# Layer 2 of two feed-forward layers: combined weights made earlier, seven products in every tile, and a new plan

## The chip, the cores and the metric

The kernel runs on one core of one Trainium2 chip. The metric is the device time of one execution in microseconds (us). The engines are TensorE (PE, matrix products; PEld is its weight load), VectorE (DVE), ScalarE (ACT), GpSimd (POOL) and SyncE (SP), which issues almost all DMAs in one in-order queue.

## The reference, cut to what matters

```python
# attention: 2 x 8 heads, 768 positions, 64 wide; a local window of 16 on either side,
# and 24 block summaries (max of k, mean of v over 32 positions)
a = np.exp(scores_all); a = a / (np.sum(a, axis=-1, keepdims=True) + 1e-09)
x = np.matmul(a, v_all)            # as 1536 tokens x 512
# layer 1 (called layer 0 in the code)
h = x @ w_in                       # 512 x 2048
x = (h * (1.0 / (1.0 + np.exp(-1.702 * h)))) @ w_out
# layer 2 (layer 1 in the code)
h = x @ w_in2
out = (h * np.cos(h)) @ w_out2
```

## The kernel before

**Tiles and steps.** The 1536 tokens are three tiles of 512 (`U`). Each layer goes through its tiles one after the other, and each tile in 16 steps f of 128 hidden columns. A step computes h on TensorE (`ff_h`, L881), passes it through a gate chain of ScalarE and VectorE (`ff_gate`, L996; 2 links in layer 1, 7 in layer 2), splits the result into g hi and g lo, and multiplies it by w_out into four accumulators (`ff_out`, L1093), two steps behind. Every fp32 product is three fp32r passes over hi and lo parts (hi x hi, lo x hi, hi x lo). The attention of the second and third tile (units 4 to 11 of 128 positions) is laid between the steps of layer 1's first two tiles; at the start, 13 dummy products and more behind the first units keep TensorE busy (`fill`, L383).

**Weights.** Each weight row m is 1 MB of raw 64-bit words for two blocks. `w_load` (L725) brings it into one of the buffers rawA, rawB, rawC; `convert` (L737) makes the two blocks' hi and lo parts: scale (L740, ACT), low (L746, DVE), join (L750, DVE), and for each block hi (L767, ACT) and lo (L771, DVE). Layer 1's 16 rows are converted during its first tile, layer 2's 16 rows during its third.

**Combined products.** For the second and third tile of layer 2 (`WINO`), two steps are taken together as a pair: `ff_wino` (L913) computes their h by a seven-product scheme for 2 x 2 blocks in place of eight, each product six matmuls of 256 columns (L939). It takes blocks of w and x (1 to 4) and combined ones: sums of weight blocks, and sums t1 to t4 of x blocks (`prep_wino`, L836). Sums of the products ("h copy" on ACT, L962; seven "h sum" on DVE, L964) give the four blocks of h. The first tile of layer 2 has plain steps.

**Where the weight sums come from.** In `convert` of the eight rows with w_in blocks, `sums_of` (L787) follows the join: four sums (L794, DVE), hi (L798, ACT), lo (L799, DVE), all in the row's own raw buffer, and a 1 MB DMA to a DRAM scratch (`sd`, L802). So the raw buffer is free for the next row's load only when that DMA has landed. In layer 2 each pair loads its 1 MB back (L925).

**Buffers.** xf0 and xf1 hold a tile's x or output ([128, 4, 512]); `xb` holds seven slots of split x. rawC holds the attention's k, q, v (`win`) until the last unit. `stage` and `spare` take the two buffers of the ring "wc" from layer 2's second tile on.

**Order.** All work is recorded as `Op`s; `order_of` (L271) sorts them with estimated durations and a table of priorities (`BONUS`), and each engine runs its instructions in that order, waiting on semaphores.

## Time and profile before

| what | us |
|---|---|
| three runs | 601.88, 603.9, 604.45; median 603.9 |
| the profiled execution, its time | 602.34 |
| its span, first to last instruction | 600.6 |
| time around the span | 1.74 |
| TensorE busy in the span | 580.6 (97%) |
| TensorE's mean granted clock | 0.995 of full speed |

A profile tells of one execution. Busy shares are averages over stages with different limits: what a change is worth is read from the waits in its stage. The stages are: start and first attention units to about 32 us, layer 1's first tile to 147, its second to 230, its third to about 337, then layer 2's three tiles of some 80 us each.

### The profile page before, as it was taken

Reading aid. Unit: us, or ns where it says so; the run is one execution under the profiler, and the core shown is the slowest. Engines: PE = TensorE matmul, PEld = TensorE weight load, DVE = VectorE, ACT = ScalarE, POOL = GpSimd, SP = SyncE. Lnnn points to the kernel's source line nnn. Section 1 sums busy time; section 2 is a strip of 40 time slices with the busy share of each in tenths; the row PEclk is TensorE's granted clock in tenths of the full one; section 3 lists DMA queues with packets and bytes.
Section 4 is the critical chain, followed back from the end, with each engine's and each line's share of the span. In section 5 each row is a group of like instructions: output and inputs, shape, how many; then the busy total and the mean of one; then the engine's idle time right before and its main releaser. Section 6 shows DMA issues by size and latency. Waiting matters only on the chain.

```text
span 600.6 us, 9453 instructions
## 1 busy us (share of the span) xinstructions
PE 580.6 (97%) x3628; PEld 479.4 (80%) x3633; DVE 431.0 (72%) x879; ACT 362.5 (60%) x733; POOL 29.9 (5%) x30
## 2 busy tenths in 40 slices
...
GB/s 326 395 344 244 196 198 266 217 108 175 8 73 80 36 0 141 211 210 204 207 220 210 280 1 1 0 1 0 113 204 105 71 76 135 141 136 76 1 2 70
DMA packets 27789, 82.30 MB, mean 137 GB/s; under 512 B 10336, under 2 KB 15456, under 8 KB 20576
## 3 DMA queue, kind: packets, MB, share of 16 engines
...
q14 instruction: 17, 0.14, 0.1%
q10 hardware_dynamic: 144, 0.13, 0.1%
...
## 4 chain that ended last, share of the span: by engine, by line
PE 62%; DVE 16%; DMA 15%; ACT 4%; issue 2%; SPq 1%; POOL 0%; DVEq 0%
PE acc L1108 30%; PE h_ps L894 19%; PE h_ps L939 8%; DMA raw<-in_w_dram 7%; DMA sd<-raw 5%; DMA vy<-in_vext_dram 2%; PE x_ps L541 2%; DVE g L1041 2%; DVE w L771 2%; DVE spare L964 1%; DVE gt L1033 1%; DVE raw L746 1%; DVE h_ps L964 1%; DVE raw L799 1%; PE s_ps L512 1%
## 5 line engine op out<-in xcount | busy, mean ns | idle before, releaser
L1108 PE MATMUL acc<-g,w 128*128 128x512 f32 x1155 | 279.6, 391 | 2.5 <-DVE g L1041 2.5
L1108 PEld LDWEIGHTS acc<-g,w 128*128 128x128 f32 x1155 | 213.6, 188 | 47.1 <-DVE g L1041 4.2
L894 PE MATMUL h_ps<-xb,w 128*128 128x512 f32 x768 | 187.8, 395 | 4.9 <-DVE gt L1009 2.8
L894 PEld LDWEIGHTS h_ps<-xb,w 128*128 128x128 f32 x768 | 143.5, 189 | 39.0 <-DVE gt L1009 5.1
L1037 ACT CAST g<-gt 128x512 fp32r<-128x512 f32 x96 | 59.3, 617 | 47.6 <-PE acc L1108 41.8
L1041 DVE TENSOR_TENSOR g<-gt,g 128x512 fp32r<-128x512 f32 x96 | 66.9, 698 | 27.6 <-ACT g L1037 27.3
L939 PE MATMUL h_ps<-xb,sums 128*128 128x256 f32 x384 | 52.6, 284 | 1.8 <-DVE h_ps L964 1.8
L939 PEld LDWEIGHTS h_ps<-xb,sums 128*128 128x128 f32 x384 | 49.2, 191 | 4.3 <-DVE h_ps L964 2.7
L1025 ACT ACTIVATE gt<-gt 128x512 f32<-128x512 f32 x48 | 30.2, 630 | 36.5 <-DVE gt L1021 36.4
L1003 ACT ACTIVATE gt<-h_ps 128x512 f32<-128x512 f32 x48 | 28.7, 597 | 34.5 <-PE h_ps L894 21.0
L1005 ACT ACTIVATE gt<-h_ps 128x512 f32<-128x512 f32 x48 | 28.6, 597 | 33.5 <-DVE g L1041 22.7
L771 DVE TENSOR_TENSOR w<-wc,w 128x512 fp32r<-128x512 f32 x64 | 46.9, 742 | 1.5 <-ACT w L767 1.5
L740 ACT ACTIVATE wc<-raw 128x1024 f32<-128x1024 f32 x32 | 36.8, 1155 | 14.5 <-DMA raw<-in_w_dram 8.8
L1033 DVE SCALAR_TENSOR_TENSOR gt<-gt,h_ps 128x512 f32<-128x512 f32 x48 | 32.8, 682 | 16.4 <-ACT gt L1029 16.4
L767 ACT CAST w<-wc 128x512 fp32r<-128x512 f32 x64 | 37.9, 619 | 8.9 <-DVE wc L750 4.7
L939 PE MATMUL h_ps<-xb,w 128*128 128x256 f32 x288 | 41.2, 284 | 1.5 <-DVE spare L964 1.2
L750 DVE SCALAR_TENSOR_TENSOR wc<-wc,raw 128x1024 uint32<-128x1024 uint32 x32 | 39.6, 1242 | 3.7 <-ACT wc L740 3.6
L939 PEld LDWEIGHTS h_ps<-xb,w 128*128 128x128 f32 x288 | 38.3, 191 | 4.0 <-ACT gt L1025 1.4
L1009 DVE SCALAR_TENSOR_TENSOR gt<-gt,h_ps 128x512 f32<-128x512 f32 x48 | 32.7, 681 | 11.4 <-ACT gt L1003 11.2
L1017 DVE SCALAR_TENSOR_TENSOR spare<-gt,h_ps 128x512 f32<-128x512 f32 x32 | 21.9, 685 | 20.8 <-ACT gt L1013 20.7
L746 DVE TENSOR_SCALAR raw<-raw 128x1024 uint32<-128x1024 uint32 x32 | 23.2, 725 | 14.9 <-DMA raw<-in_w_dram 14.9
L1013 ACT ACTIVATE gt<-gt 128x512 f32<-128x512 f32 x48 | 30.4, 633 | 1.5
...
## 6 DMA issues: line engine op xcount, KB each, us to landing
raw<-in_w_dram SPq DMA_DIRECT2D x32, 1024.0 KB, 5.8
sums<-sd SPq DMA_DIRECT2D x16, 1024.0 KB, 4.8
sd<-raw SPq DMA_DIRECT2D x8, 1024.0 KB, 4.0
...
```

Of the source, the lines that this page charges most:

```text
L740: nc.scalar.activation(out=t.bitcast(FP32), in_=raws[m][:, :, 1].bitcast(FP32), func=ACTF.Prelu, scale=REBIAS, alpha=SIGN)
L750: nc.vector.scalar_tensor_tensor(out=t, in0=t, scalar=3, in1=raws[m][:, :, 0], op0=ALU.logical_shift_left, op1=ALU.bitwise_or)
L767: nc.scalar.copy(out=w[:, 0, :], in_=mids[m][:, 512 * a:512 * (a + 1)].bitcast(FP32))
L771: nc.vector.tensor_tensor(out=w[:, 1, :], in0=mids[m][:, 512 * a:512 * (a + 1)].bitcast(FP32), in1=w[:, 0, :].bitcast(FP32), op=ALU.subtract,)
L894: nc.tensor.matmul(out=hs[i], lhsT=w[:, a, c], rhs=x[:, b, :], start=(k == 0 and n == 0), stop=(k == KD - 1 and n == 2),)
L939: nc.tensor.matmul(out=half(dst), lhsT=wts(a)[:, 128 * k:128 * (k + 1)], rhs=x[:, b, k, :], start=k == a == b == 0, stop=k == b == 1,)
L1009: nc.vector.scalar_tensor_tensor(out=gt, in0=gt, scalar=1.0, in1=hs[i], op0=ALU.add, op1=ALU.mult)
L1013: nc.scalar.activation(out=gt, in_=gt, func=ACTF.Copy, bias=-MAGIC)
L1033: nc.vector.scalar_tensor_tensor(out=gt, in0=gt, scalar=0.5, in1=hs[i], op0=ALU.subtract, op1=ALU.mult)
L1037: nc.scalar.copy(out=g[:, 0, :], in_=gts[i])
L1041: nc.vector.tensor_tensor(out=g[:, 1, :], in0=gts[i], in1=g[:, 0, :].bitcast(FP32), op=ALU.subtract)
L1108: nc.tensor.matmul(out=accs[d][:, c], lhsT=w[:, a, 128 * d:128 * (d + 1)], rhs=g[:, b, c], start=(f == 0 and n == 0), stop=(f == NF - 1 an ...
```

## The change

**What it does.** (1) `sums_ahead` (new) takes the place of `sums_of`: it loads the eight rows with w_in blocks once more, in layer 1's second tile (i = 16), converts them to the joined fp32 only, makes the same sums and puts them to `sd`. Even rows use rawB, odd rows x slots 2 and 3, which that tile doesn't use and which are now a tile of their own (`x23`). The ordinary conversion in the third tile stays, without sums. (2) All pairs of layer 2 but the first (`NPLAIN` = 1) of its first tile now use the seven products: 7 + 8 + 8 pairs instead of 8 + 8. (3) The products of a pair stand in another order, with other accumulator halves: 1, 3, 6, 7, 5, 2, 4 where it was 1, 5, 6, 7, 2, 3, 4; products 7 and 5 now wait for the sum u2 behind product 6, and product 4 for o22. (4) `x_sums` makes t1 to t4 in place in xf, so `stage` is gone; `spare` and the gate's buffer r lie over the attention's constants (`cst`), which are not needed by then. (5) Layer 1's last output has rawC as its buffer, not xf0. (6) The last tile's evacuation: DVE, ACT, DVE, ACT, the last one whole with its store in two halves; before, the last one was in two halves on both engines. (7) The planner's table and a few of its durations are new, so the order changes everywhere.

```diff
-WINO = {(1, 1), (1, 2)}
+NPLAIN = 1
+SLOTS = {"11": 5, "12": 6, "21": 2, "22": 3, "t1": 4, "t2": 0, "t3": 1, "t4": 6}
...
-PE_DEFAULT = 3 * U
+PE_DEFAULT = 3 * U / 0.68
...
-        return 0.13 if a == "DVE" else 0.0
+        return {"DVE": 0.13, "DMA": 2.27}.get(a, 0.0)
...
-        if m >= NF and c == 0:
-            sums_of(m, f // 2, o4, rr, wr)
...
+    def sums_ahead(p):
+        m, st = NF + ROWS.index(p), {}
+        rings = ("rawB",) if p % 2 == 0 else ("x2", "x3")
...
+        def load():
+            if p % 2 == 0:
+                st["raw"] = raw_p.tile([128, 2048], U32, name="ahead", tag="rawB")
+            else:
+                st["raw"] = mid_slots(U32, "ahead").rearrange("p s n -> p (s n)")
+            nc.sync.dma_start(out=st["raw"], in_=w2[m - NF].bitcast(U32))
...
+        wr = ring["wc"]
+        ld = use(op("load w", "DMA", 2.65, load), True)
+        o1 = use(wr.take(op("w scale", "ACT", 1.06, scale, ld)))
+        o2 = use(op("w low", "DVE", 0.6, lambda: nc.vector.tensor_scalar(
+            out=part(0), in0=part(0), scalar1=29, scalar2=None, op0=ALU.logical_shift_right), ld))
+        prior = use(wr.use(op("w join", "DVE", 1.14, lambda: nc.vector.scalar_tensor_tensor(
+            out=st["mid"], in0=st["mid"], scalar=3, in1=part(0), op0=ALU.logical_shift_left, op1=ALU.bitwise_or), o1, o2)))
         for k, x, y, sign in ((0, lambda: a(2), lambda: a(3), ALU.add), (2, lambda: a(0), lambda: a(2), ALU.subtract),
                               (1, lambda: a(3), lambda: at(2), ALU.subtract), (3, lambda: a(1), lambda: at(1), ALU.subtract)):
-            prior = op("w sum", "DVE", 0.34, lambda k=k, x=x, y=y, sign=sign: nc.vector.tensor_tensor(
-                out=at(k), in0=x(), in1=y(), op=sign), prior)
-            rr.use_of(raw_rec[m], prior)
-            wr.use(prior)
-        oh = op("s hi", "ACT", 1.04, lambda: nc.scalar.copy(out=whole()[:, 0:1024], in_=whole()[:, 1024:2048].bitcast(FP32)), prior)
-        ol = op("s lo", "DVE", 1.14, lambda: nc.vector.tensor_tensor(
+            prior = use(wr.use(op("w sum", "DVE", 0.34, lambda k=k, x=x, y=y, sign=sign: nc.vector.tensor_tensor(
+                out=at(k), in0=x(), in1=y(), op=sign), prior)))
+        oh = use(op("s hi", "ACT", 0.98, lambda: nc.scalar.copy(
...
+        ol = use(op("s lo", "DVE", 1.14, lambda: nc.vector.tensor_tensor(
...
+        s_put[p] = use(op("put s", "DMA", 1.8, lambda: nc.sync.dma_start(out=sd[p], in_=whole().bitcast(FP32)), ol))
...
+    def x_slot(layer, t, k):
+        if (layer, t, k) == (1, 0, "t4"):
+            return NX
+        return SLOTS[k] if layer else ((0, 1, 2, 3), (4, 5, 6, 0), (2, 3, 1, 4))[t][k]
...
+    def x_sums(t, names):
+        key = (1, t)
+        b = lambda i, j: xf_of(key)[:, 2 * i - 2:2 * i, HU * (j - 1):HU * j]
...
+        for k in names:
+            if k in ("11", "12", "21", "22"):
+                split((1, t, k), lambda k=k: b(int(k[0]), int(k[1])), *half(int(k[0])))
+            elif k == "t1":
+                take(k, lambda: b(1, 2), lambda: b(1, 2), lambda: b(1, 1), *half(1), *x_ready.get((1, t, "12"), ()))
+            elif k == "t2":
+                take(k, lambda: b(2, 2), lambda: b(2, 2), lambda: b(1, 2), x_sum[t, "t1"], *x_ready[1, t, "22"])
+                split((1, t, k), lambda: b(2, 2), x_sum[t, "t2"])
+            elif k == "t3":
+                take(k, lambda: b(1, 1), lambda: b(2, 2), lambda: b(1, 1), x_sum[t, "t2"], *x_ready[1, t, "11"])
+                split((1, t, k), lambda: b(1, 1), x_sum[t, "t3"])
+            elif k == "s1":
+                split((1, t, "t1"), lambda: b(1, 2), x_sum[t, "t1"])
+            elif k == "t4":
+                take(k, lambda: b(2, 1), lambda: b(2, 1), lambda: b(2, 2), x_sum[t, "t2"], *x_ready[1, t, "21"])
+                split((1, t, k), lambda: b(2, 1), x_sum[t, "t4"])
...
-        a = op("alloc", "POOL", 0.0, spare_of)
-        if not ring["spare"].held:
-            ring["wc"].take(a)
-        ring["spare"].take(a)
-        y, u, v = lambda: p1_sb, lambda: spare[0][:, U:U + HU], lambda: spare[0][:, U + HU:2 * U]
-        p1 = product(2, lambda a: w(0, a), 0, A)
-        s1 = both(y, lambda: half(A), None, a, p1)
-        p5 = product(1, lambda a: sums(0, a), 1, D)
-        p6 = product(1, lambda a: sums(1, a), 2, E)
-        u2 = both(u, y, lambda: half(E), s1, p6)
-        u4 = both(v, u, lambda: half(D), u2, p5)
-        p7 = product(1, lambda a: sums(2, a), 3, C)
-        u7 = both(lambda: half(E), v, lambda: half(C), u4, p7)
-        u3 = both(u, u, lambda: half(C), u4, p7)
-        p2 = product(1, lambda a: w(1, a), 4, A)
-        p2.deps.append(s1)
-        o11 = both(lambda: half(A), y, lambda: half(A), p2)
-        p3 = product(1, lambda a: sums(3, a), 5, D)
-        p3.deps.append(u4)
-        o12 = both(lambda: half(D), v, lambda: half(D), p3)
-        p4 = product(1, lambda a: w(3, a), 6, C)
-        p4.deps.extend([u7, u3])
-        o21 = both(lambda: half(C), u, lambda: half(C), p4)
+        u, v = (cst[:, U + HU * k:U + HU * (k + 1)] for k in range(2))
+        p1 = product(lambda a: w(0, a), "11", A)
+        p3 = product(lambda a: sums(3, a), "22", D)
+        s1 = op("h copy", "ACT", 0.27, lambda: nc.scalar.copy(out=p1_sb, in_=half(A)), p3)
+        ring["u"].take(s1)
+        ring[tags[0]].use_of(h_rec[i], s1)
+        p6 = product(lambda a: sums(1, a), "t2", E)
+        u2 = both(lambda: u, lambda: p1_sb, lambda: half(E), s1, p6, *late)
+        p7 = product(lambda a: sums(2, a), "t3", C, u2)
+        p5 = product(lambda a: sums(0, a), "t1", E, u2)
+        u3 = both(lambda: v, lambda: u, lambda: half(C), u2, p5)
+        u4 = both(lambda: u, lambda: u, lambda: half(E), u3)
+        o22 = both(lambda: half(E), lambda: v, lambda: half(E), u4)
+        p2 = product(lambda a: w(1, a), "21", A, s1)
+        o12 = both(lambda: half(D), lambda: u, lambda: half(D), u4, p2)
+        o11 = both(lambda: half(A), lambda: p1_sb, lambda: half(A), p2)
+        p4 = product(lambda a: w(3, a), "t4", C, o22)
+        o21 = both(lambda: half(C), lambda: v, lambda: half(C), p4)
         ff_gate(i, [o11, o12])
-        ff_gate(i + 1, [o21, u7])
+        ff_gate(i + 1, [o21, o22])
...
-            r = rs[0] = spare[0][:, 0:U] if wino else bank("a1", "r")[:, 0:U]
+            r = rs[0] = cst[:, 0:U]
...
+        if i + 2 == NU:
+            late.append(vput[-1])
...
-            at = (i // (NF * NTU), i // NF % NTU)
-            if i % NF == 0 and i:
-                prep_wino(at[1]) if at in WINO else prep(*at)
-            if at in WINO:
+            layer, t, f = i // (NF * NTU), i // NF % NTU, i % NF
+            if i == NF:
+                for p in range(NP):
+                    sums_ahead(p)
+            if f == 0 and layer == 0 and t:
+                prep(t)
+            if layer and f == 0:
+                x_sums(t, ("11", "22", "t1", "t2", "t3", "s1", "21", "t4") if t else ("11", "12", "21", "22", "t1", "t2", "t3"))
+            if layer and t == 0 and f == 2 * NPLAIN:
+                x_sums(t, ("s1", "t4"))
+            if layer and (t or f >= 2 * NPLAIN):
                 if i % 2 == 0:
                     ff_wino(i)
             else:
```

**SP's queue, layer 1's third tile.** First the kernel before: the end of the attention's loads and the first weight loads (L728) and puts of sums (L802) of layer 2's rows.

```order
L446 DMA win<-in_kT_dram 128x4x96 x2
L363 DMA win<-in_qT_dram 128x4x128
L363 DMA win<-in_vext_dram 128x1024
L728 DMA raw<-in_w_dram 128x2048 x2
L802 DMA sd_91<-raw 128x2048
L728 DMA raw<-in_w_dram 128x2048 x2
L802 DMA sd_92<-raw 128x2048
L728 DMA raw<-in_w_dram 128x2048 x2
```

Now the same place in the changed kernel, from the last load of attention q on; L821 and L848 are the loads and puts of `sums_ahead`, L970 the loads of sums.

```order
L382 DMA win<-in_qT_dram 128x4x128
L821 DMA ahead<-in_w_dram 128x2048
L848 DMA sd_94<-ahead 128x2048
L750 DMA raw<-in_w_dram 128x2048
L848 DMA sd_95<-ahead 128x2048
L382 DMA win<-in_vext_dram 128x1024
L750 DMA raw<-in_w_dram 128x2048 x15
L970 DMA sums<-sd_89 128x2048
```

Loads and puts took turns in the third tile; now the last put stands in front of it, and 15 weight loads follow one another.

**VectorE, the sums.** The kernel before at the end of layer 1's third tile: sums (L794), low (L746), w lo (L771), join (L750), s lo (L799), g lo (L1041) and layer 2's first gate links (L1017, L1021).

```order
L794 TENSOR_TENSOR raw<-wc,raw 128x256
L746 TENSOR_SCALAR raw<-raw 128x1024
L794 TENSOR_TENSOR raw<-wc,raw 128x256
L1041 TENSOR_TENSOR g<-gt,g 128x512
L746 TENSOR_SCALAR raw<-raw 128x1024
L771 TENSOR_TENSOR w<-wc,w 128x512
L799 TENSOR_TENSOR raw<-raw 128x1024
L1017 SCALAR_TENSOR_TENSOR r<-gt,h_ps 128x512
L750 SCALAR_TENSOR_TENSOR wc<-wc,raw 128x1024
L1021 SCALAR_TENSOR_TENSOR gt<-gt,r 128x512
L1041 TENSOR_TENSOR g<-gt,g 128x512
L771 TENSOR_TENSOR w<-wc,w 128x512 x2
```

In the changed kernel the sums (L841), low (L835), join (L837) and s lo (L845) stand in the second tile, between that tile's gates (L1052) and g lo (L1084).

```order
L845 TENSOR_TENSOR ahead<-ahead 128x1024
L835 TENSOR_SCALAR ahead<-ahead 128x1024
L1084 TENSOR_TENSOR g<-gt,g 128x512
L1052 SCALAR_TENSOR_TENSOR gt<-gt,h_ps 128x512
L837 SCALAR_TENSOR_TENSOR wc<-wc,ahead 128x1024
L841 TENSOR_TENSOR ahead<-wc 128x256 x2
L1052 SCALAR_TENSOR_TENSOR gt<-gt,h_ps 128x512
L841 TENSOR_TENSOR ahead<-wc,ahead 128x256 x2
L845 TENSOR_TENSOR ahead<-ahead 128x1024
L1084 TENSOR_TENSOR g<-gt,g 128x512
L835 TENSOR_SCALAR ahead<-ahead 128x1024
```

And this is layer 2's start in the changed kernel: gate links (L1060, L1064, L1076), g lo (L1084), joins and w lo (L772, L793), an x lo (L871), an evacuation (L1172).

```order
L1060 SCALAR_TENSOR_TENSOR cst<-gt,h_ps 128x512
L772 SCALAR_TENSOR_TENSOR wc<-wc,raw 128x1024
L1084 TENSOR_TENSOR g<-gt,g 128x512
L1064 SCALAR_TENSOR_TENSOR gt<-gt,cst 128x512
L793 TENSOR_TENSOR w<-wc,w 128x512 x2
L1060 SCALAR_TENSOR_TENSOR cst<-gt,h_ps 128x512
L1064 SCALAR_TENSOR_TENSOR gt<-gt,cst 128x512
L1076 SCALAR_TENSOR_TENSOR gt<-gt,h_ps 128x512
L871 TENSOR_TENSOR wc<-xf,wc 128x512
L1076 SCALAR_TENSOR_TENSOR gt<-gt,h_ps 128x512
L1172 TENSOR_SCALAR xf<-acc_2640 128x512
L1084 TENSOR_TENSOR g<-gt,g 128x512
```

At the end of the third tile no sum and no s lo is left between the gates.

**TensorE, one pair of the seven products.** The kernel before, second tile of layer 2: product 4 of the pair ahead and 1 (x12), 5 and 6 (x12), half an `ff_out` step, 7, 2, 3.

```order
L939 MATMUL h_ps<-xb,w 128x256 x12
L939 MATMUL h_ps<-xb,sums 128x256 x12
L1108 MATMUL acc_3990<-g,w 128x512
L1108 MATMUL acc_3992<-g,w 128x512
L1108 MATMUL acc_3990<-g,w 128x512
L1108 MATMUL acc_3992<-g,w 128x512
L1108 MATMUL acc_3990<-g,w 128x512
L1108 MATMUL acc_3992<-g,w 128x512
L939 MATMUL h_ps<-xb,sums 128x256 x6
L939 MATMUL h_ps<-xb,w 128x256 x6
```

The changed kernel, first tile: product 4 of the pair ahead, 1, 3 (`x_2424` is `x23`), 6, half an `ff_out` step, 7 and 5.

```order
L986 MATMUL h_ps<-wc,w 128x256 x6
L986 MATMUL h_ps<-xb,w 128x256 x6
L986 MATMUL h_ps<-x_2424,sums 128x256 x6
L986 MATMUL h_ps<-xb,sums 128x256 x6
L1147 MATMUL acc_3296<-g,w 128x512
L1147 MATMUL acc_3298<-g,w 128x512
L1147 MATMUL acc_3296<-g,w 128x512
L1147 MATMUL acc_3298<-g,w 128x512
L1147 MATMUL acc_3296<-g,w 128x512
L1147 MATMUL acc_3298<-g,w 128x512
L986 MATMUL h_ps<-xb,sums 128x256 x12
```

The half step of six accumulator products now stands between 6 and 7, behind which the sums of 7 and 5 follow.

## Rows read from the trace of the kernel before

**Rows 1.** The page of the kernel before: busy time and instructions of each engine.
```profile
PE 580.6 (97%) x3628; PEld 479.4 (80%) x3633; DVE 431.0 (72%) x879; ACT 362.5 (60%) x733; POOL 29.9 (5%) x30
```

**Rows 2.** Stretches: start:end, length, busy PE, PEld, DVE, ACT, POOL, clock, DMA, GB/s.
```profile
32.00:66.00 34.00, 31.05 (x176) 23.91 (x175) 32.51 (x55) 21.23 (x45) 11.96 (x8) 1.00 0.72 257
66.00:147.00 81.00, 80.94 (x583) 65.57 (x582) 70.28 (x161) 57.95 (x137) 5.43 (x6) 1.00 0.62 207
147.00:230.00 83.00, 83.00 (x571) 68.47 (x570) 29.26 (x88) 32.34 (x88) 3.10 (x3) 1.00 0.13 38
...
293.00:341.00 48.00, 42.81 (x176) 33.11 (x176) 40.54 (x65) 32.14 (x49) 0.00 (x0) 0.98 0.64 238
341.00:418.00 77.00, 77.00 (x338) 63.68 (x337) 46.21 (x73) 46.59 (x79) 0.00 (x0) 0.99 0.05 19
418.00:597.00 179.00, 175.03 (x1079) 156.06 (x1078) 132.15 (x257) 107.85 (x191) 0.00 (x0) 1.00 0.26 91
```

**Rows 3.** Waits of TensorE's matmuls, whole span: us in total, times, longest us.
```profile
PE h_ps L894 <- DVE gt L1009: 2.8, 4, 1.4
PE acc L1108 <- DVE g L1041: 2.5, 4, 1.1
PE h_ps L894 <- DVE gt L1033: 2.1, 1, 2.1
PE h_ps L939 <- DVE h_ps L964: 1.8, 2, 0.9
PE h_ps L939 <- DVE spare L964: 1.2, 1, 1.2
```

**Rows 4.** All engines' waits from 230 to 345 us: us in total, times, longest.
```profile
DVE raw L746 <- DMA raw<-in_w_dram: 10.3, 7, 3.2
```

**Rows 5.** The chain that ended last, 325 to 360 us: start, duration, what.
```profile
324.05 4.76 DMA raw<-in_w_dram
...
330.12 1.22 DVE raw L799
...
331.94 1.14 DVE wc L750
...
337.62 4.44 PE h_ps L894 x12
...
354.51 2.72 PE h_ps L894 x12
```

**Rows 6.** By shape, 230 to 341 us: count, busy us, mean ns, idle before.
```profile
L771 DVE TENSOR_TENSOR w<-wc,w 128x512 fp32r<-128x512 f32 x30 | 20.3, 684 | 0.4 <-ACT w L767 0.4
...
L750 DVE SCALAR_TENSOR_TENSOR wc<-wc,raw 128x1024 uint32<-128x1024 uint32 x15 | 18.1, 1219 | 1.8 <-ACT wc L740 1.8
...
L746 DVE TENSOR_SCALAR raw<-raw 128x1024 uint32<-128x1024 uint32 x14 | 9.7, 692 | 10.3 <-DMA raw<-in_w_dram 10.3
L799 DVE TENSOR_TENSOR raw<-raw 128x1024 fp32r<-128x1024 f32 x7 | 8.5, 1221 | 0.5 <-ACT raw L798 0.5
...
L794 DVE TENSOR_TENSOR raw<-wc 128x256 f32<-128x256 f32 x14 | 5.8, 417 | 0.0
```

**Rows 7.** The page's DMA issues: count, KB of one, median us to landing.
```profile
raw<-in_w_dram SPq DMA_DIRECT2D x32, 1024.0 KB, 5.8
...
sd<-raw SPq DMA_DIRECT2D x8, 1024.0 KB, 4.0
```

**Rows 8.** The chain that ended last, whole span: a run of combined products.
```profile
530.14 4.31 PE h_ps L939 x36
```

**Rows 9.** VectorE by shape, all: a sum of two product halves.
```profile
L964 DVE TENSOR_TENSOR spare<-spare,h_ps 128x256 f32<-128x256 f32 x32 | 13.3, 417 | 1.7 <-PE h_ps L939 1.2
```

**Rows 10.** VectorE by shape, 52 to 62 us.
```profile
L771 DVE TENSOR_TENSOR w<-wc,w 128x512 fp32r<-128x512 f32 x2 | 3.5, 1760 | 0.0
```

**Rows 11.** All engines in order of time, 584 us to the end: the last two evacuations.
```profile
595.64 1.09 ACT L1076 ACTIVATE xf<-acc 128x512 f32<-128x512 f32 x2 [0.76 <-PE acc L1108]
...
596.77 0.42 DVE L1078 TENSOR_SCALAR xf<-acc 128x256 f32<-128x256 f32 x1 [1.11 <-ACT xf L1076]
```

More of the change, by code (lines that the diff above doesn't have):

```diff
@@ L716, in xf_op @@
             o.deps.append((r.held[xf_rec[key]][0],))
+    order, late, x_sum = [], [], {}
     wt, raws, mids = {}, {}, {}
@@ L799, in sums_of @@
-        ol = op("s lo", "DVE", 1.14, lambda: nc.vector.tensor_tensor(
-            out=whole()[:, 1024:2048], in0=whole()[:, 1024:2048].bitcast(FP32), in1=whole()[:, 0:1024].bitcast(FP32),
-            op=ALU.subtract), oh)
-        put = op("put s", "DMA", 2.65, lambda: nc.sync.dma_start(out=sd[p], in_=whole().bitcast(FP32)), ol)
-        for o in (oh, ol, put):
-            rr.use_of(raw_rec[m], o)
-        s_put[p] = put
-    hs, gts, gs, rs, accs, x_rec, h_tags, stage, spare = {}, {}, {}, {}, {}, {}, {}, [], []
@@ new lines, in local_global_attention_two_ffn, with split, hi @@
+    hs, gts, gs, rs, accs, x_rec, h_tags = {}, {}, {}, {}, {}, {}, {}
+    o_prev, h_prev, g_last = [None], [None], {}
+    def x_slot(layer, t, k):
+        if (layer, t, k) == (1, 0, "t4"):
+            return NX
+        return SLOTS[k] if layer else ((0, 1, 2, 3), (4, 5, 6, 0), (2, 3, 1, 4))[t][k]
+    def split(key, src, *deps):
+        n = x_slot(*key)
+        place = lambda a: xs(n)[:, a, :].rearrange("p (k n) -> p k n", k=2) if key[0] else xs(n)[:, a, :]
+        def hi():
+            if key == (0, NTU - 1, 0):
+                mid_slots(F32R)
+            if n == NX:
+                x_last[0] = wc_p.tile([128, 1024], F32R, name="wc", tag="wc")
+            nc.scalar.copy(out=place(0), in_=src())
+        oh = op("x hi", "ACT", 0.52, hi, *deps)
+        ol = op("x lo", "DVE", 0.6, lambda: nc.vector.tensor_tensor(
+            out=place(1), in0=src(), in1=place(0).bitcast(FP32), op=ALU.subtract), oh)
+        ring[f"x{n}"].take(oh)
+        ring[f"x{n}"].use(ol)
+        x_rec[key] = n, len(ring[f"x{n}"].held) - 1
+        x_ready[key] = [ol]
+        for o in (oh, ol):
+            xf_op(key[0:2], o, False)
+        return ol
@@ L914, in ff_wino @@
         t, f = i // NF % NTU, i % NF
-        p, q = f // 2, sum(1 for x in WINO if x[1] < t) * NP + f // 2
+        p, q = f // 2, len(order)
+        order.append(i)
         tags = ("a0", "a1") if q % 2 else ("h", "h")
```

261 lines of the change are left out of this document (122 added, 139 removed), and 162 rows, old and new, of the table BONUS.

## The prediction

> **What bounds the kernel now.** I read the engine line of the page first: TensorE is busy 580.6 of 600.6 us [rows 1]. A change can therefore win in three ways only: fewer products, less of the 20 us in which TensorE stands, or less time at half clock. The stretches tell where it stands [rows 2]. Layer 1's first two tiles leave nothing (80.94 of 81.00 us and 83.00 of 83.00), but the end of the third tile with layer 2's first steps (293 to 341 us) loses 48.00 − 42.81 = 5.2 us, the two tiles of combined products lose 179.00 − 175.03 = 4.0, and the start (32 to 66 us) loses 34.00 − 31.05 = 3.0. The waits say for whom: the matmuls of h and of the accumulators wait for VectorE's gate links, and in two places each for sums of products [rows 3].
>
> VectorE is only the messenger in the third tile. Between 230 and 345 us it waited 10.3 us, in 7 places, for a raw weight row to land [rows 4]. The chain ahead of the worst stop shows the link [rows 5]: a weight row's DMA (4.76 us) that ends at 328.8, then VectorE's s lo (1.22) and join (1.14), then TensorE's h at 337.62. That load is late because the raw buffer holds the sums until their 1 MB put has landed, and a put takes 4.0 us to land, a load 5.8 [rows 7]. On top of it the run of 12 matmuls behind this stop took 4.44 us, where the same run at 354.51 took 2.72 [rows 5]: the granted clock of that stretch is 0.98 against 1.00 [rows 2], so part of the run went at 1.2 GHz after TensorE had waited.
>
> **The change, part by part.**
>
> *Products.* A plain pair is two steps of h, 2 × 2.72 = 5.44 us [rows 5]. A combined pair is 42 matmuls; 36 of them take 4.31 us [rows 8], so 42 × 4.31 / 36 = 5.03. Seven more pairs: 7 × 0.41 = **−2.9 us**.
>
> *Third tile without sums.* What goes from 230 to 341 us is, for each of eight rows, four sums at 0.417 and an s lo at 1.221 [rows 6], 2.89 us, so 23 us of VectorE, and on SP's queue the eight puts that alternated with the loads. The order of the change shows 15 loads one behind the other. With two buffers in turn and no put, a load of 5.8 us has a whole row's time to land; a row now costs VectorE a low, a join and two lo, 0.69 + 1.22 + 2 × 0.68 = 3.3 us [rows 6], and 16 rows are spread over 83 us or more. The 5.2 us could go altogether. I keep 1.4 of them: two VectorE links of some 0.69 (an x lo and an evacuation still stand among layer 2's first gate links, as the order shows). **−3.8 us**, bounds 0 and −5.2.
>
> *Half clock.* If the stop goes, so does 4.44 − 2.72 = **−1.7 us**; if a stop of about 2 us stays there, it stays.
>
> *Second tile of layer 1 with the sums.* Each row costs VectorE a low, a join, four sums and an s lo: 0.69 + 1.22 + 4 × 0.417 + 1.22 = 4.8 us [rows 6], eight rows 38 us. The tile's VectorE is busy 29.26 of 83 us [rows 2], so 68 of 83 after it. That is near the first tile, where 70.28 of 81.00 cost TensorE 0.06 us. ScalarE gets a scale and a hi for each row; at 1.22 us each as a ceiling that is 20 us on 32.34 of 83. What is queued behind a join on VectorE is a gate link, and for that TensorE waits: a gate is two steps ahead of its use, which is two times two runs of 2.72 us, against 1.22 for the longest instruction ahead of it. The SP queue holds now eight loads and eight puts more, 16 MB; the DMA share of that tile is 0.13 [rows 2], and a buffer's round trip of 4.0 + 5.8 us [rows 7] is met by two buffers (10 us for two rows, while 83 us are there for eight). The loads of the attention's k, q, v that stand behind a put in the queue can be held up by it. I take **+0.5**; bounds 0 and 5.2 (the same stop as in the third tile).
>
> *Order of the products.* The seven-product pairs cost TensorE 1.8 + 1.2 = 3.0 us of waits in 16 pairs now [rows 3]. In the new order product 7 waits for u2, made from product 6: between them stands half a step of the accumulators, six matmuls, half of 2.72 = 1.36 us, against one sum of 0.417 [rows 9] and at most one gate link or lo of 0.68 in front of it. This covers it, with 0.3 us to spare. Product 4 waits for o22, three sums behind product 5 (3 × 0.417 = 1.25), with product 2 (0.72) and half a step between. I keep the 3.0 us: **0**, bounds −3.0 and, at about 1 us a pair, a rival below.
>
> *Sums of x and of products in layer 2's first tile.* Its VectorE goes up from 46.21 of 77.00 us by seven pairs of seven sums, 49 × 0.417 = 20.4, and by sums and lo parts of x, some 5.5 (8 × 0.69), to 72 of 74 if nothing else changed. But 46.21 holds the last conversions and seven rounds of plain work of its own; the two tiles that carry all of this have 132.15 of 179.00, 74% [rows 2], and lose 4.0 us in two tiles. I take 0 more than the kept waits. This is the thinnest cover in the sum; if it is gone, it costs what the other tiles lose, up to 2.0.
>
> *Tail, start and plan.* The last evacuation is now one whole instruction on ScalarE in place of two halves on both engines: before, 1.09 us for two on ScalarE, so 0.55 each, then 0.42 on VectorE [rows 11]. The difference is within ±0.2; 0. The new table moves the start too; the 3.0 us that TensorE loses there could go or double, and nothing in the trace says which: 0, bounds ±3.0. The own buffer for layer 1's last output takes a wait on a buffer away that no row shows as TensorE's: 0.
>
> **Sum:** −2.9 − 3.8 − 1.7 + 0.5 = **−7.9 us**. The durations are those of one execution of 602.34 us (span 600.6 and 1.74 around it), which gives 594.4. That execution is 1.6 below the median of the runs, 603.9; against the median I say **596.0**.
>
> **Rivals.**
>
> *The stop moves into layer 1's second tile.* The same low, join, sums and put run there, with 4.0 us put and 5.8 us load per buffer. Against it: 83 us for eight rows rather than 16, and two buffers used by nothing else. For it: this tile has no slack on TensorE at all, so each late gate shows. It pays 5.2 − 1.4 + 1.7 − 0.5 = 5.0 again: 601.0.
>
> *All waits go.* The plan and the order of products also take away the product waits, the residue and the half microsecond: 596.0 − 3.0 − 1.4 − 0.5 = 591.1. For it: the six-matmul cover, and that TensorE's 83.00 of 83.00 shows a tile can run without a gap.
>
> *Slower: product 7 or 4 waits in each pair.* If the gate links on VectorE stand ahead of u2 or o22 and are late, each pair waits as the three shown did, 3.0 / 3 = 1.0 us [rows 3]. Times 23 pairs, 23 us in place of the 3.0 kept: 616. It decides the sign from (3.0 + 7.9 + 3.0) / 23 = 0.6 us a pair. Against it: in 16 pairs only three such waits were there, and the covers worked out above. Because u, v and r now lie in one buffer, a sum that waits for an earlier reader of u would have the same effect.
>
> *GpSimd and VectorE get in each other's way.* VectorE's lo of a block took 1760 ns [rows 10] from 52 to 62 us, inside the stretch in which GpSimd is busiest (11.96 of 34.00 us from 32 to 66 [rows 2]), against 684 ns later [rows 6]. In layer 1's second tile GpSimd is busy 3.10 us in 3 instructions [rows 2], and the sums now lie beside them. If each of its microseconds holds VectorE up and TensorE with it: 596.0 + 3.1 = 599.1. The Trainium skill, page "SBUF — State Buffer", section "SBUF: two separate sides", describes the shared port pair of the two engines as an exclusive lock, in which an operation of VectorE with two SBUF inputs and one of GpSimd that reads SBUF keep each other out for a whole instruction. The row of 1760 ns agrees with that rule; no row tells which of the two held the ports.
>
> *The change does nothing:* if the third tile's stop had another cause, the products alone stay, 603.9 − 2.9 = 601.0, as the first rival; it is counted with it.
>
> **How the numbers follow.** About 0.5%, 3.0 us, is what a measurement of this kernel can tell from no change, so faster begins below 600.9. The forecast has 0.55, with its own range of 592.5 to 600.0 (3.5 below for the start's 3.0 and the tail, 4.0 above for the bounds of the second tile); the moved stop (or another cause) 0.14, no waits left 0.20, GpSimd 0.06, slower 0.05. Faster: 0.53 of the forecast, 0.20, 0.05 of GpSimd and 0.05 of the moved stop, whose 601.0 lies at the bound: 0.83. Same: 0.12, the rest of the moved stop (0.09), of the forecast (0.02) and of GpSimd (0.01). Slower: 0.05. The range goes from 589.5, 1.6 below the case without waits, to 601.5, just above the moved stop; what lies above and below it is 0.05 of the slower case and some 0.10 of tails.
>
> **What would show it.** Right, if after the change VectorE waits for raw rows by less than 2 us in layer 1's third tile, TensorE stands there for about 1.4 us instead of 5.2, the run of 12 matmuls at the change of layers takes 2.72, the second tile keeps its full TensorE, the seven added pairs each take 5.0 and TensorE's busy time falls by about 2.9 + 1.7 = 4.6 us. Wrong, if matmuls of h or of the accumulators wait for the sums in the second tile; if matmuls of the products wait for sums in more than a few pairs; or if the first weights or x sums of layer 2 are late at its start, which no row of before can show.

## The result, and the profile after

The changed kernel takes 585.11 us (median of 4 runs, 584.2 to 585.36); the kernel before took 602.89 on the same chip. The ratio is 0.9709, with a 95% interval of 0.9665 to 0.9753. That is 17.8 us faster; the prediction said 7.9 us faster, and the fast end of its range was 589.5.

The page and the stretches of the profiled execution after (span 583.2 us), in the columns of [rows 1] and [rows 2]:

```profile
PE 572.3 (98%) x3751; PEld 482.7 (83%) x3756; DVE 471.6 (81%) x952; ACT 374.4 (64%) x751; POOL 29.4 (5%) x30
```

```profile
32.00:66.00 34.00, 32.14 (x202) 25.36 (x203) 31.81 (x55) 22.95 (x50) 12.17 (x8) 1.00 0.69 252
147.00:228.00 81.00, 81.00 (x562) 66.60 (x561) 62.49 (x139) 48.32 (x106) 3.10 (x3) 1.00 0.67 245
228.00:290.00 62.00, 62.00 (x275) 51.34 (x274) 44.54 (x63) 34.23 (x53) 0.00 (x0) 1.00 0.37 133
290.00:333.00 43.00, 43.00 (x200) 35.95 (x199) 37.62 (x56) 31.72 (x51) 0.00 (x0) 1.00 0.44 166
333.00:403.00 70.00, 69.25 (x437) 62.53 (x436) 56.22 (x111) 43.01 (x77) 0.00 (x0) 1.00 0.30 106
403.00:580.00 177.00, 176.27 (x1088) 158.43 (x1087) 139.27 (x266) 112.78 (x198) 0.00 (x0) 1.00 0.28 98
```

Layer 1's third tile (228 to 333) has no gap left, and its clock is 1.00 throughout. The second tile took up 33 us more of VectorE (62.49 of 81.00 against 29.26 of 83.00) without one either. Layer 2's last two tiles stand for 0.7 us instead of 4.0. TensorE's waits of 0.5 us or more after, in the columns of [rows 3]:

```profile
PE wps L403 <- POOL p_sb L399: 1.1, 1, 1.1
PE h_ps L932 <- DVE gt L1052: 1.1, 1, 1.1
PE t_ps L586 <- ACT ex L545: 0.8, 1, 0.8
PE h_ps L986 <- DVE cst L1012: 0.7, 1, 0.7
PE acc L1147 <- DVE g L1084: 0.6, 1, 0.6
PE x_ps L560 <- DVE xb L631: 0.5, 1, 0.5
PE x_ps L560 <- issue: 0.5, 1, 0.5
```

The products' matmuls wait for a sum (L986 for L1012) only once, at the change of layers; a run of 24 of them in the chain that ended last (start, duration, what):

```profile
338.62 2.87 PE h_ps L986 x24
```

VectorE waits from 228 to 345 us, as in [rows 4], 3.3 us for raw rows instead of 10.3:

```profile
DVE raw L768 <- DMA raw<-in_w_dram: 3.3, 3, 2.4
```

**A count by the starts of matmuls.** Busy time hides part of a stop, because a matmul counts as busy until its modelled end. So I took, for every matmul of h, of the products and of the accumulators, the time from its start to the start of the next matmul of any kind, less the usual spacing (0.227 us with 512 columns, 0.120 with 256; the medians of both kernels). The sum is what TensorE lost behind these matmuls, by waiting and by half clock. By tile, cut at each 192nd accumulator matmul (a stop ahead of a tile's first accumulator matmul counts in the tile before), for all runs of this study (one profiled execution each, us):

```
run                      start+   tile 2   tile 3 | layer 2:               all
                         tile 1                   | tile 1  tile 2  tile 3
before                     6.7      1.4      9.0  |  0.1     3.7     1.9    22.9
after                      4.5      1.7      0.0  |  1.6     0.5     0.6     8.9
e1  old product order      4.7      1.7      0.0  |  3.2     2.7     1.9    14.2
e2  old table              6.6     11.0      0.2  |  3.2     0.7     0.7    22.5
e3  plain tile             6.1      2.4      0.1  |  0.6     0.5     0.6    10.2
e4  before, new table      3.3      1.8      1.8  |  0.5     2.2     1.9    11.5
e5  before, no sums        5.7      1.4      0.0  |  0.1     3.7     1.9    12.9
e6  before, no puts        6.0      1.4      1.0  |  0.3     3.7     1.9    14.4
e7  before, puts only      5.4      1.4      3.5  |  0.1     3.7     1.9    16.0
e8  sums in third tile     3.8      1.7      1.9  |  2.9     0.4     1.1    11.9
e9  before, new products   4.9      1.4      8.6  |  3.6     0.6     0.1    19.1
e10 plain tile, pinned     1.9      1.8      0.1  |  0.6     0.5     0.7     5.6
```

The first two rows answer the first question: 14.0 of the 17.4 us between the two spans are time that TensorE no longer loses, 9.0 of them in layer 1's third tile, 4.5 in layer 2's second and third tile, and 2.2 at the start; 1.5 go back in layer 2's first tile and 0.3 in layer 1's second. Another 2.9 are the products (294 matmuls of 0.120 in place of 168 of 0.227); 0.5 is left unassigned. The first column is rough, because what stands behind matmuls of the attention is not in it: the last accumulator matmul of layer 1's first tile starts at 150.2 us before, and in e4 only 1.1 us earlier, where the column says 3.4; in e3 it starts 4.8 us later than after, where the column says 1.6.

### The profile page after: what moved, and what is told of

The parts are those of the page before. It is cut to its first block, busy times and chain, and to the rows that moved or that the text cites. A ratio compares the mean times of both kernels' runs of the same rounds, so it can differ in the third digit from the quotient of the medians.

```text
span 583.2 us, 9825 instructions
## 1 busy us (share of the span) xinstructions
PE 572.3 (98%) x3751; PEld 482.7 (83%) x3756; DVE 471.6 (81%) x952; ACT 374.4 (64%) x751; POOL 29.4 (5%) x30
## 4 chain that ended last, share of the span: by engine, by line
PE 88%; ACT 5%; DVE 4%; DMA 2%; issue 0%; SPq 0%; ACTq 0%
PE acc L1147 42%; PE h_ps L932 21%; PE h_ps L986 19%; ACT ex L545 2%; PE x_ps L560 2%; DMA raw<-in_w_dram 2%; PE s_ps L531 1%; PE t_ps L658 1%; DMA kf<-in_kT_dram 1%; DVE g L1084 1%; DVE wc L772 1%; ACT at_early L598 0%; ACT wc L762 0%; ACT w L789 0%; PE vs_ps L505 0%
## 5 line engine op out<-in xcount | busy, mean ns | idle before, releaser
L932 PE MATMUL h_ps<-xb,w 128*128 128x512 f32 x396 | 98.2, 393 | 1.1 <-DVE gt L1052 1.1
L932 PEld LDWEIGHTS h_ps<-xb,w 128*128 128x128 f32 x396 | 73.5, 188 | 18.4 <-DVE gt L1052 1.9
L1084 DVE TENSOR_TENSOR g<-gt,g 128x512 fp32r<-128x512 f32 x96 | 68.3, 711 | 18.5 <-ACT g L1080 17.5
L986 PE MATMUL h_ps<-xb,sums 128*128 128x256 f32 x414 | 57.1, 283 | 0.7 <-DVE cst L1012 0.7
L986 PEld LDWEIGHTS h_ps<-xb,sums 128*128 128x128 f32 x414 | 54.3, 191 | 3.0 <-DVE cst L1012 1.2
L793 DVE TENSOR_TENSOR w<-wc,w 128x512 fp32r<-128x512 f32 x64 | 46.2, 735 | 10.0 <-ACT w L789 10.0
L932 PE MATMUL h_ps<-x,w 128*128 128x512 f32 x204 | 52.1, 390 | 0.0
L1060 DVE SCALAR_TENSOR_TENSOR cst<-gt,h_ps 128x512 f32<-128x512 f32 x48 | 32.9, 685 | 15.1 <-ACT gt L1056 14.5
L932 PEld LDWEIGHTS h_ps<-x,w 128*128 128x128 f32 x204 | 38.2, 188 | 8.1 <-issue 0.2
L772 DVE SCALAR_TENSOR_TENSOR wc<-wc,raw 128x1024 uint32<-128x1024 uint32 x32 | 40.5, 1275 | 2.5 <-ACT wc L762 2.4
L1068 ACT ACTIVATE gt<-gt 128x512 f32<-128x512 f32 x48 | 30.3, 631 | 17.2 <-DVE gt L1064 17.1
L1076 DVE SCALAR_TENSOR_TENSOR gt<-gt,h_ps 128x512 f32<-128x512 f32 x48 | 32.8, 684 | 9.1 <-ACT gt L1072 9.1
L1052 DVE SCALAR_TENSOR_TENSOR gt<-gt,h_ps 128x512 f32<-128x512 f32 x48 | 32.7, 681 | 2.6 <-ACT gt L1046 2.3
L1012 DVE TENSOR_TENSOR h_ps<-cst,h_ps 128x256 f32<-128x256 f32 x69 | 28.4, 424 | 7.6 <-PE h_ps L986 7.4
L1064 DVE SCALAR_TENSOR_TENSOR gt<-gt,cst 128x512 f32<-128x512 f32 x48 | 33.1, 689 | 0.8
```

The lines of the kernel that those rows point to most:

```text
L772: nc.vector.scalar_tensor_tensor(out=t, in0=t, scalar=3, in1=raws[m][:, :, 0], op0=ALU.logical_shift_left, op1=ALU.bitwise_or)
L793: nc.vector.tensor_tensor(out=w[:, 1, :], in0=mids[m][:, 512 * a:512 * (a + 1)].bitcast(FP32), in1=w[:, 0, :].bitcast(FP32), op=ALU.subtract,)
L932: nc.tensor.matmul(out=hs[i] if layer == 0 else hs[i].rearrange("p (j n) -> p j n", j=2), lhsT=w[:, a, c], rhs=rhs(b), start=(k == 0 and n ...
L986: nc.tensor.matmul(out=half(dst), lhsT=wts(a)[:, 128 * k:128 * (k + 1)], rhs=x[:, b, k, :], start=k == a == b == 0, stop=k == b == 1,)
L1060: nc.vector.scalar_tensor_tensor(out=r, in0=gts[i], scalar=-C1, in1=hs[i], op0=ALU.mult, op1=ALU.add)
L1064: nc.vector.scalar_tensor_tensor(out=gt, in0=gt, scalar=-C2, in1=rs[0], op0=ALU.mult, op1=ALU.add)
```

## The experiments

**The two kernels with one part undone or done alone: products and table.**

e1: the old order of the products in the changed kernel.

```diff
         p1 = product(lambda a: w(0, a), "11", A)
-        p3 = product(lambda a: sums(3, a), "22", D)
...
+        p5 = product(lambda a: sums(0, a), "t1", D)
         p6 = product(lambda a: sums(1, a), "t2", E)
...
-        p7 = product(lambda a: sums(2, a), "t3", C, u2)
-        p5 = product(lambda a: sums(0, a), "t1", E, u2)
...
+        p7 = product(lambda a: sums(2, a), "t3", C)
+        o22 = both(lambda: half(E), lambda: v, lambda: half(C), u4, p7)
...
         p2 = product(lambda a: w(1, a), "21", A, s1)
...
+        p3 = product(lambda a: sums(3, a), "22", D, u4)
...
-        p4 = product(lambda a: w(3, a), "t4", C, o22)
+        p4 = product(lambda a: w(3, a), "t4", C, o22, u3)
```

> The changed kernel (585.1 us) with the old order of the products of a pair: 1, 5, 6, 7, 2, 3, 4, where 7 follows 6 at once and 3 and 4 wait for sums just made; all 23 pairs, sums in layer 1's second tile, the new table. Theory P: layer 2 lost about 6 us before (16 pairs) and about 1 us after because of this order, so 5 us or more come back with 23 pairs: 590 to 593 us, and TensorE's matmuls wait for sums of products in many pairs. Theory T: the order of all instructions that the new table sets did it: 585 to 587 us, and few such waits.

Measured: 590.92 us (590.41 to 592.98), ratio to before 0.9792 (0.9754 to 0.9831), 5.8 more than the changed kernel (5.0 by the ratios; each round of runs has its own of the kernel before, with medians of 602.4 to 603.4 us). All of it lies in layer 2, which loses 7.8 us by the count and not 2.7. TensorE's waits from 320 us on:

```profile
PE h_ps L986 <- DVE h_ps L1012: 1.4, 2, 0.9
PE h_ps L986 <- DVE cst L1012: 1.3, 2, 1.1
PE acc L1147 <- ACT g L1080: 0.7, 1, 0.7
```

Theory P holds for the size, and only in part for the form. By these rows the products wait in four places; counted by starts, eight of the 23 pairs lose 0.35 to 1.4 us each.

What the old order waits for can be read in the kernel before, behind the waits of [rows 3]. TensorE, one stop at product 3 and one at product 2 of a pair, and VectorE ahead of each:

```profile
493.24 0.98 PE L939 MATMUL h_ps<-xb,sums 128*128 128x256 f32 x6 [0.88 <-DVE h_ps L964]
510.93 0.95 PE L939 MATMUL h_ps<-xb,w 128*128 128x256 f32 x6 [1.19 <-DVE spare L964]
```

```profile
492.77 0.42 DVE L964 TENSOR_TENSOR h_ps<-p_sb,h_ps 128x256 f32<-128x256 f32 x1
510.36 0.42 DVE L964 TENSOR_TENSOR spare<-spare,h_ps 128x256 f32<-128x256 f32 x1
```

Product 3 waited for the sum made from product 2 (the other half of its bank), here and in one more pair, 1.1 us each by starts; product 2 for a sum made from product 5, 1.4 us here and 0.2 to 0.3 in three more pairs. Product 4 lost 0.35 us in each of two pairs to a sum made from product 7. In the new order product 3 follows product 1 and waits for no sum of its pair.

e2: the old table in the changed kernel. `BONUS` is that of the kernel before, and:

```diff
-        return {"DVE": 0.13, "DMA": 2.27}.get(a, 0.0)
+        return 0.13 if a == "DVE" else 0.0
-PE_DEFAULT = 3 * U / 0.68
+PE_DEFAULT = 3 * U
...
-                columns = PE_COLUMNS.get(o.kind if o.kind in PE_COLUMNS else o.kind.split()[-1], PE_DEFAULT * o.dur)
+                columns = PE_COLUMNS.get(o.kind if o.kind in PE_COLUMNS else o.kind.split()[-1], PE_DEFAULT)
```

> The changed kernel with the planner's old table of priorities, its old lag for DMAs and its old column count; all else as changed. Theory P (structure): only the start comes back, 2.4 us, so 587 to 588.5 us, with layer 2 and the end of layer 1 without waits. Theory T (table): the start and layer 2's waits come back, 2.4 + 5, so 592 us or more.

Measured: 598.24 us (597.04 to 598.66), ratio 0.9894 (0.9856 to 0.9932). Neither theory: layer 2's waits do not come back in its second and third tile, as P said, but layer 1's second tile now loses 11.0 us. Stretches of that run around the place, and its ScalarE and TensorE in order of time (start, duration, engine, line, what, idle before):

```profile
147.00:168.00 21.00, 21.00 (x152) 17.29 (x152) 14.34 (x24) 8.68 (x14) 0.00 (x0) 1.00 0.47 159
168.00:178.00 10.00, 5.59 (x15) 3.97 (x13) 6.54 (x24) 5.90 (x19) 1.99 (x1) 0.71 0.86 312
```

```profile
171.32 1.17 ACT L830 ACTIVATE wc<-ahead 128x1024 f32<-128x1024 f32 x1 [2.47 <-DMA ahead<-in_w_dram]
172.37 0.59 ACT L707 COPY xf<-x_ps 128x512 f32<-128x512 f32 x1
...
173.01 3.35 PE L932 MATMUL h_ps<-xb,w 128*128 128x512 f32 x7 [4.41 <-ACT xf L707]
```

This is the prediction's first rival, caught in the act. A scale of the early sums (L830) stands at the head of ScalarE's queue and waits 2.47 us for its row; behind it stands the copy (L707) that empties the bank of the next h; TensorE waits 4.41 us, and the granted clock of the stretch is 0.71. The row is late because its buffer's put took 8.64 us, and the load behind it 5.27, in the chain that ended last:

```profile
157.37 8.64 DMA sd<-ahead
...
166.02 5.27 DMA ahead<-in_w_dram
```

That put was issued 0.4 us behind the load of another row. In the changed kernel each put stands 3.6 us or more behind the last weight load, and takes 3.8 to 5.0 us. SP in e2:

```profile
156.93 0.33 SPq L821 DMA_DIRECT2D ahead<-in_w_dram  x1
157.37 0.37 SPq L848 DMA_DIRECT2D sd<-ahead  x1
```

e4: the new table in the kernel before, the same three places the other way round.

> The kernel before (602.9 us) with the planner's new table, lag and column count alone. Theory P (structure): the start gains up to 2.4 us, the rest stays: 600 to 603 us, with VectorE still waiting for weight rows in the third tile and matmuls for sums of products. Theory T (table): the layer 2 waits go too: 595 us.

Measured: 593.69 us (592.05 to 597.95), ratio 0.9843 (0.979 to 0.9895), 9.7 us faster than before. Both theories missed it: layer 2 keeps its waits (4.6 of 5.7 us), but the third tile, with all its sums and puts, loses 1.8 us and not 9.0. VectorE waited there 1.1 us for raw rows in place of 10.3 [rows 4]:

```profile
DVE raw L746 <- DMA raw<-in_w_dram: 1.1, 2, 0.8
```

The trace gives the times. The third and fourth load of layer 2's rows are issued at 223.3 and 223.8 us, 5.1 us earlier than before (228.4 and 228.9), and the low of the last row starts at 323.1 in place of 328.9. So the sequence takes 100 us in either kernel, and with the old order it ended when layer 2's first gates wanted VectorE. SP's queue, from 225 to 345 us, shows what it waits for: most of all its puts wait for VectorE's s lo (L799), and loads for puts; the latter is what the new table shortened. First before, then e4:

```profile
SPq L802 <- DVE raw L799: 54.0, 7, 11.0
SPq L728 <- DMA sd<-raw: 23.6, 6, 7.1
```

```profile
SPq L802 <- DVE raw L799: 61.8, 7, 15.4
SPq L728 <- DMA sd<-raw: 8.4, 3, 3.6
```


**The stop in layer 1's third tile.** Three runs of the kernel before with its old table. In each, layer 2 loads parts of layer 1's weights from the scratch, put there in the second tile, so that no sum is needed; the edit is the same but for what it leaves in the third tile: e5 no `sums_of`, e6 `sums_of` without its put, e7 its put alone, to another scratch.

```diff
+        if i == NF:
+            for p in range(NP):
+                def early_put(p=p):
+                    for k in range(2):
+                        nc.sync.dma_start(out=sd[p][:, 1024 * k:1024 * (k + 1)], in_=wt[0, 1, p].rearrange("p a n -> p (a n)").bitcast(FP32))
+
+                s_put[p] = op("put s", "DMA", 2.65, early_put, w_ready[0, 1, p], h_of[NF - 1][-1])
+                ring["w1"].use_of(w_rec[0, 1, p], s_put[p])
```

> The kernel before, old table, without the weight sums in layer 1's third tile: what layer 2 loads in their place are parts of layer 1's weights, put to the scratch in layer 1's second tile, so that the output is not the reference's. No sum, s hi, s lo and no put is left in the third tile. Theory S (sums and puts make the stop there, as predicted): the 9.0 us lost in that tile go, 603 - 7 = 594 to 598 us. Theory T (the old order makes it, whatever the sums): 600 to 603 us, with VectorE still waiting for weight rows.

> As the run without sums, but the sums, s hi and s lo stay in the third tile and only the eight puts are gone (layer 2 loads the same parts of layer 1's weights, so the output is not the reference's). If the puts, which hold the raw buffers and take turns with the loads, make the stop: 594 to 598 us, as without sums. If VectorE's 23 us of sums make it: 600 to 603 us.

> The opposite: no sums, s hi and s lo in the third tile, but eight puts of 1 MB from the raw buffers behind each join, to a scratch that nobody reads (layer 2 loads parts of layer 1's weights; the output is not the reference's). If the puts make the stop: 599 to 603 us. If VectorE's sums make it: 594 to 598 us.

Measured: 593.27 us without sums (591.91 to 595.01), ratio 0.9835 (0.9791 to 0.9879); 596.23 with sums and no puts (592.85 to 596.76), 0.9867 (0.9825 to 0.9908); 595.9 with puts and no sums (594.89 to 599.42), 0.9884 (0.9839 to 0.9928). Before was 603.23. Theory S holds for e5, with a time just under its range. In the third tile they lose 0.0, 1.0 and 3.5 us in place of 9.0, while layer 2's second and third tile stay at 3.7 and 1.9 in all three. Taking both away is worth the whole 9.0; taking either away is worth most of it (8.0 the puts, 5.5 the sums; by the medians of the times the two are alike, 7.0 and 7.3). So e6 came out as if the puts made the stop, and e7 as if the sums did: it is both in a row, join, sums, s lo, put, next load, that overran. VectorE's wait for rows isn't the measure, as the run with puts alone shows; it waited more than before and cost TensorE 5.5 us less:

```profile
DVE raw L746 <- DMA raw<-in_w_dram: 12.4, 9, 3.2
```

Its puts are not quite those of before, though. They need no sums, six of the seven in the third tile were issued 0.4 us behind a load, and these took 8.4 to 9.8 us to land; before, a put took 4.0 [rows 7]. So 3.5 us may be more than such puts cost where they stood.

```profile
se<-raw SPq DMA_DIRECT2D x8, 1024.0 KB, 8.5
```

e8: the changed kernel with `sums_of` in the third tile again.

```diff
-            if i == NF:
-                for p in range(NP):
-                    sums_ahead(p)
...
+        if m >= NF and c == 0:
+            sums_of(m, f // 2, o4, rr, wr)
```

> The changed kernel (585.1 us), new table, with the sums made in layer 1's third tile again, in the raw buffer with its put, and no second load of weights. Theory S (the place of the sums is worth 5.5 to 7 us): 590.5 to 592 us. Theory T (with the new table the third tile loses 1.8 us even with the sums in it, as in the run of the kernel before with the new table): 586 to 588 us.

Measured: 589.81 us (588.15 to 590.47), ratio 0.9768 (0.9734 to 0.9803), 4.7 more than the changed kernel (3.6 by the ratios): between the two theories. By the count the third tile loses 1.9 us more and layer 2's first tile 1.3 (the profiled execution was the fastest of the four; the rest was not seen). Of the 1.9, 1.1 stand among layer 2's first products, which the cut counts in the third tile; TensorE's waits from 325 to 350 us:

```profile
PE h_ps L1008 <- DVE cst L1034: 1.4, 1, 1.4
PE h_ps L1008 <- DVE gt L1098: 0.7, 1, 0.7
```

So with the new table the place of the sums is worth 3 to 5 us, not 9, less than one of them in the third tile's own steps, and the rest at the change of layers.

**Products alone, and the plain tile.**

e9: the new order of the products in the kernel before (the lines of e1 the other way round).

> The kernel before (603 us), old table, 16 pairs, sums in the third tile, with the new order of the products of a pair (1, 3, 6, 7, 5, 2, 4) alone. Theory P (the order of the products takes layer 2's waits away): of the 5.7 us that its matmuls lose in layer 2, counted by their starts, 1 to 2 are left, so 598.5 to 600 us. Theory T (it needs the new table): 602 to 605 us.

Measured: 600.81 us (598.18 to 604.46, 10 runs), ratio 0.9971 (0.9948 to 0.9995): faster by 1.6 us, a little over what can be told apart from nothing, and between the two theories. By the count layer 2 still loses 4.3 of its 5.7 us. Its second and third tile lose 0.6 + 0.1 us, not 3.7 + 1.9, as theory P said of the pairs; but the second combined pair pays: its product 4 waits 1.9 us for the sums behind product 5, with a stretch of lower clock behind it (0.72); by the cut of the tiles this counts in the first one (3.6). The wait (the only one of that run from 345 us on), the stop with the matmuls ahead of it, VectorE's work ahead of it, and the stretches:

```profile
PE h_ps L939 <- DVE h_ps L964: 1.9, 1, 1.9
```

```profile
427.72 1.59 PE L939 MATMUL h_ps<-xb,sums 128*128 128x256 f32 x12
429.15 0.88 PE L939 MATMUL h_ps<-xb,w 128*128 128x256 f32 x6
431.88 2.02 PE L939 MATMUL h_ps<-xb,w 128*128 128x256 f32 x12 [1.85 <-DVE h_ps L964]
```

```profile
426.95 0.42 DVE L964 TENSOR_TENSOR spare<-p_sb,h_ps 128x256 f32<-128x256 f32 x1 [0.24 <-issue]
...
429.21 0.69 DVE L1134 TENSOR_SCALAR xf<-acc 128x512 f32<-128x512 f32 x1
429.81 0.41 DVE L964 TENSOR_TENSOR spare<-spare,h_ps 128x256 f32<-128x256 f32 x1
430.14 0.68 DVE L1034 SCALAR_TENSOR_TENSOR gt<-gt,h_ps 128x512 f32<-128x512 f32 x1
430.74 0.42 DVE L964 TENSOR_TENSOR spare<-spare,h_ps 128x256 f32<-128x256 f32 x1
```

```profile
425.00:431.00 6.00, 5.03 (x37) 4.57 (x35) 5.69 (x11) 5.21 (x11) 0.00 (x0) 1.00 0.52 199
431.00:437.00 6.00, 5.12 (x27) 5.03 (x28) 4.50 (x11) 3.99 (x8) 0.00 (x0) 0.72 0.61 204
437.00:590.00 153.00, 153.00 (x941) 137.40 (x941) 117.19 (x225) 95.32 (x167) 0.00 (x0) 1.00 0.23 83
```

u2 (426.95) was in time for product 7 (427.72). Then product 2 alone stood between products 5 and 4, with no half step, and on VectorE an evacuation (L1134) and a gate link (L1034) stood ahead of and among the sums. From 437 us on TensorE does not stand once: 153.00 of 153.00 us. In the changed kernel the first pair of layer 2 waits 0.7 us, and there it is product 7 that waits for u2.

e3 and e10: plain steps in all of layer 2's first tile; in e10 the operations of layer 1 are also held in the order of the changed kernel, by a list.

```diff
-NPLAIN = 1
+NPLAIN = 8
...
-                x_sums(t, ("11", "22", "t1", "t2", "t3", "s1", "21", "t4") if t else ("11", "12", "21", "22", "t1", "t2", "t3"))
+                x_sums(t, ("11", "22", "t1", "t2", "t3", "s1", "21", "t4") if t else ("11", "12", "21", "22"))
```

> The changed kernel with plain steps in all of layer 2's first tile (eight plain pairs, none of seven products; sums of x are not made there). By the prediction's sum seven pairs at 0.41 us are lost: 585.1 + 2.9 = 588.0 us, and nothing else changes. Rival: the first tile's pairs also cost VectorE so much that they are worth less, so 585.5 to 587 us; or the change of layers is worse with plain steps, as before, and it is 590 us or more.

> The changed kernel with plain steps in all of layer 2's first tile, as in the first such run, but now with the instructions of layer 1 held in the changed kernel's order until shortly before layer 2 (the first such run had an order of its own there, with a wait of 2.3 us in the first tile). By the prediction's term for seven pairs: 585.1 + 2.9 = 588.0 us; with the 1.0 us that the first tile's matmuls then lose less, as the first such run showed, 587.0 us. If the plain tile itself costs more, 589 us or more as before.

Measured: 590.38 us (587.77 to 592.47), ratio 0.9775 (0.9726 to 0.9823), and pinned 587.08 us (584.9 to 587.45), ratio 0.9746 (0.972 to 0.9773). The first is in the range of its second rival, but says little: its planner gave layer 1 another order, with a wait of 2.3 us in the first tile and a granted clock of 0.72 from 113 to 119 us. Pinned, the cost is 2.0 us: 2.9 of products less the 1.0 us that the plain tile loses less (0.6 for 1.6). That is what its expectation said; its four runs are themselves 2.6 us apart.

## Why the prediction was wrong, step by step

- **Products, −2.9: right.** A run of 24 such matmuls takes 2.87 us after, 0.1196 each; e10 agrees, with 2.9 less 1.0.
- **Third tile, −3.8, and half clock, −1.7: the mechanism right, the size wrong, and the cause shared.** The step that failed is "I keep 1.4 of them", and the 5.2 us under it. Nothing of the stop stayed, and it had cost 9.0, not 5.2 + 1.7: the stretch's idle time leaves out what the modelled ends of matmuls cover. e5 to e7 show that puts and sums in a row made it. But e4 shows that the new table removes 7.2 of the same 9.0 with the sums in place. Either takes most of it, so their gains do not add: 10.0 us without sums on the old table, 9.7 for the table alone, and with the new table 4.7 for the place (e8). Two of the prediction's signs fail here: VectorE still waits 3.3 us for raw rows, not less than 2, without a stop of TensorE behind it, and TensorE's busy time falls by 8.3 us, not 4.6.
- **Order of the products, 0: wrong.** The step is "I keep the 3.0 us". I worked out that the new order covers u2 with 0.3 us to spare, and took that for no change, without working out what the old order covered: there products 2, 3 and 4 each have a sum of their own pair to wait for, and products 2 and 3 lost most. The new one was worth 4.5 us in layer 2's second and third tile (e9: 4.9; e1: 3.5 back in these two, 5.1 in all three). Here too the rows of waits (3.0) understate the loss (5.6). The rival of a late product 4 came true in one pair of e9, where the half step that the prediction counts between products 2 and 4 was not there; so with the old table the order was worth 1.6 us net.
- **Second tile, +0.5: right for this table only.** It lost 0.3 us more. With the old table the first rival comes true, 11.0 us (e2). The prediction gave the mechanism 0.14 and saw it on VectorE; it struck on ScalarE, by a scale that waits at the head of the queue.
- **Layer 2's first tile, 0 with a bound of 2.0: mis-sized** at +1.5 us, 0.7 of it the first pair's wait for u2; e10 puts it at 1.0 against plain steps.
- **Start and plan, 0 within ±3.0:** −2.2 in the profiled executions. Runs with the same order there differ as much (after and e10 by 2.6 us, before and e9 by 1.8), so none of it can be told from chance.
- **The rivals.** The nearest was that all waits go, 591.1, with a chance of 0.20. Its price was too low by the same two sizes. The plan, which I could not read, was kept out of the sum apart from the start: the failure common to these steps. The collision with GpSimd (0.06) cost TensorE nothing: the second tile has the same three copies (3.10 us) and no gap. VectorE was held up all the same: two instructions of the attention (L554), the first of which started beside the copy at 195.97 us, took 2.01 us together, where one alone takes 0.66; none of the sums stood beside a copy. That agrees with the rule of the Trainium skill on the shared port pair ("SBUF — State Buffer", section "SBUF: two separate sides"). After, GpSimd and VectorE:

```profile
195.97 1.03 POOL L483 COPY win<-cst 24x1024 f32<-24x1024 f32 x1 [28.95 <-DMA win<-in_vext_dram]
196.07 2.01 DVE L554 TENSOR_TENSOR room<-room 128x480 f32<-128x480 f32 x2
...
216.54 0.66 DVE L554 TENSOR_TENSOR room<-room 128x480 f32<-128x480 f32 x1
```

What stays open: which of the table's moves took the stop out of the third tile. The earlier loads (5.1 us) and the shorter waits for puts are read from the trace of e4; no run moved them alone.
